# Attention outputs moved within their slot, and the hi/lo split of the last two ordinary weight passes dealt to other engines

## The chip, the cores and the metric

The kernel runs on one core of a Trainium2 chip. The metric is the device time of one execution in microseconds (us), lower is better; every quoted time is a median of several executions or comes from one profiled execution, and the text says which.

## The reference

An attention block with a compressive memory feeds a mixture of four dense experts.

```python
# B, H, S, D = 4, 8, 576, 64
scores = q @ k^T / 8, causal;  a = softmax(scores);  local = a @ v
q_p = elu(q) + 1
mem_out = (q_p @ M_prev) / (q_p . z_prev + 1e-6)
x = g * mem_out + (1 - g) * local          # g = sigmoid(beta), one per head
# x is laid out as 2304 rows of 512; E = 4 experts, F = 1024
out = sum over e of p[:, e] * (relu(x @ w1[e]) @ w2[e])
```

All data are 32-bit floats. The kernel keeps that precision with a split: a value is rounded to a short "hi" (type fp32r) and a remainder "lo" = value - hi, and each product is three matmuls (hi·hi, hi·lo, lo·hi).

## The kernel before, in words

**Attention as steps.** Attention is cut into tasks of two heads. A first run for batch 0 is written out by hand; then come 12 *joint* tasks (query chunks 0 and 1 of both heads, four slots each) and 16 others (five slots each). Every operation of a task is an event with a slot number and a priority within the slot; sorted by both, the events make one static list, and each engine executes its instructions in exactly that order. The table `PR` holds these slots and priorities. For a joint task that begins at slot s, the scores of its chunks (`j_qk`) stand at s and s+2 with priority 0; the output product (`j_o`) stands at s+6, and that is the third slot of the next task. In that slot of the next task one finds, by priority: `j_o` of the old task (-0.2), `j_qk` of the new task's second chunk (0), the query remainders `lo_q` of the task after that (0.4), the exponentials (6.5), the transposes of the first chunk (`j_pt`, 7). One slot earlier stand `trqp` (the transposes of the memory queries, 2.5), `lo_qp` (their remainders on VectorE, lines 371 and 374, written to `qpa` and `qpb`, 4.5) and `trq` (6.5). The PSUM tag `to` has two buffers; `trk`, `trqp`, `trq` and `j_o` take them in turn, so `j_o` takes the buffer that `trqp` had, and this one is free when `lo_qp` has read it.

**Experts as passes.** Between the steps lies the expert work. A pass `i` handles one half of one expert's F for one or two groups of 256 rows: `mm1` (line 851, 16 parts of three matmuls) and `mm2` (line 881, four parts for each block of 128 rows). The groups start at passes 0, 5, 8, 13 and 16; pass 23 is the last of this kind (`PH0` is 24). A pacing rule releases attention steps according to the TensorE cost of the parts done; a step with TensorE work counts as its cost plus 1500, another as 400.

**Weights.** `w_prep` makes hi and lo of a 128x512 piece of weights. The remainder is always a subtraction on Pool (line 249). The hi is either a copy on ScalarE (line 246) or a multiply by one on Pool (line 248). The pieces are staged by DMAs on SyncE's queue in four buffers (`stg`), and a buffer is loaded again when Pool has made its remainder.

**The last part.** From pass 22 on there are no attention steps left. During passes 22 and 23, seven operands of the remaining 1024 rows are made (`x_ops`: A11, S1, S2, S4, S3, A12, A22, each 128x1024; four of them need a sum first, line 994): `put` makes the hi on ScalarE (line 986) and the lo on VectorE (line 987). Before pass 24, `wt_prep` makes combinations of its weights twice (p = 0 and 1), with sums and remainders on VectorE (lines 1021 to 1030) and hi on ScalarE (lines 1025 to 1027). Passes 24 to 31 (the tail) then run `tail_mm1` (line 1046; products go to PSUM banks X, Y and Z, and ScalarE evicts the first of each, line 1057) and `tail_mm2` (line 1097).

Of the kernel before, what the change touches and what calls it, by code (L numbers as in the profile page):

```python
# [10 lines left out]
AF = mybir.ActivationFunctionType  # L11
# [11 lines left out]
PR = {  # L23
    "phi1": [-5, 1],
    "phi2": [-5, 7],
    "phi3": [-4, 7],
    "trq": [-3, 6.5],
    "trk": [-4, -0.5],
    "v": -2,
    "trqp": [1, 2.5],  # L30
    "qk": 0,
# [6 lines left out]
    "jn": [1, -0.45],  # L38
    "jp": [2, 7],
    "jlo": 9,  # L40
    "jo": [4, -0.2],
    "wpe": 1500,
    "wvec": 400,
    "frac": 0.97,
# [13 lines left out]
def tile_attention_moe(  # L58
# [13 lines left out]
    nc = tc.nc  # L72
# [39 lines left out]
    START = [g // 2 * NPH + (PR["x"] if g % 2 else 0) for g in range(NG)]  # L112
    PH0 = START[-1] + NPH
# [20 lines left out]
    def f(ap):  # L134
        return ap.bitcast(F32)

    def rows(c):
        return min(P, S - c * P)
# [86 lines left out]
    def w_more():  # L225

        while wpos["due"]:
            wpos["due"] -= 1
            w_dma()

    def w_prep(i, kind, pool=False):

        act = (kind == "1" or i < START[1]) and i < PH0 - PR["ahead"] and not pool
        j = wpos["prep"]
        if j >= len(wseq) or wseq[j][0] != i or wseq[j][1] != kind:
            return
        w_more()
        wpos["prep"] += 1
        fc = wseq[j][2]
        t = stg.pop(j)  # L240
        hi, lo = (w1s if kind == "1" else w2s)[fc]
        if kind == "1":
            hi = hi.rearrange("p c f -> p (c f)")
            lo = lo.rearrange("p c f -> p (c f)")
        if act:
            nc.scalar.activation(hi, t, AF.Copy)  # L246
        else:
            nc.gpsimd.tensor_scalar(hi, t, 1.0, 1.0, ALU.mult, ALU.mult)  # L248
        nc.gpsimd.tensor_tensor(lo, t, f(hi), ALU.subtract)  # L249
        wpos["due"] += 1  # L250
# [567 lines left out]
    def pcol(pieces):  # L818
        b, c = pieces[0]
        return 4 * b + c if c < 4 else 4 * B + b // 2  # L820
# [47 lines left out]
    def mm2(i, g, tt, after):  # L868
        e = halves[i][0]
        pieces = GROUPS[g][tt]  # L870
        pe = pn[:, pcol(pieces), e : e + 1]
        t0 = (g % 2) * GW + tt * P
        tk = slice(t0, t0 + P)
        pt = []

        def part(fc):
            if fc == 0:
                pt.append(ps.tile([P, 512], F32, tag="moe", name=f"y{i}_{g}_{tt}", bufs=3))
            wh, wl = w2s[fc]
            for z, (h_, w_) in enumerate(((hh, wh), (hh, wl), (hl, wh))):  # L880
                nc.tensor.matmul(  # L881
                    pt[0],
                    lhsT=h_[fc][:, tk],
                    rhs=w_,
                    start=(fc == 0 and z == 0),
                    stop=(fc == HF - 1 and z == 2),
                )
            if fc == HF - 1:
                fin()
                after()  # L890

        def fin():
            if i == START[g]:
                acc[g, tt] = sp.tile([P, DM], F32, tag="acc", name=f"acc{g}_{tt}", bufs=4)
                nc.vector.tensor_scalar(acc[g, tt], pt[0], pe, None, ALU.mult)
            else:
                nc.vector.scalar_tensor_tensor(  # L897
                    acc[g, tt], pt[0], pe, acc[g, tt], ALU.mult, ALU.add
                )
            if i == START[g] + NPH - 1:  # L900
                o0 = 0
                for b, c in pieces:
                    r0, m = b * S + c * P, rows(c)
                    nc.sync.dma_start(out=out[r0 : r0 + m, :], in_=acc[g, tt][o0 : o0 + m])
                    o0 += m

        return [lambda c=c: part(c) for c in range(HF)]

    def phase_parts(i):
        gs = [g for g in range(NG) if START[g] <= i < START[g] + NPH]  # L910
        c0 = min(g % 2 for g in gs) * GW
        cols = slice(c0, c0 + len(gs) * GW)
        out_ = []
        for fc in range(HF):
            for p_ in mm1(i, fc, cols, lambda: w_prep(i, "2")):
                out_.append((3 * mm(len(gs) * GW), p_))
        if i + 1 in START:
            out_.append((0.0, START.index(i + 1)))
        nt = 2 * len(gs)

        def after():
            if i + 1 == PH0:
                wt_prep(PH0)
            else:
                for _ in range(HF // nt):
                    w_prep(i + 1, "1")

        for g in gs:
            for tt in range(2):
                for p_ in mm2(i, g, tt, after):  # L930
                    out_.append((3 * mm(DM), p_))
        return out_
# [43 lines left out]
    def a_blk(i, k):  # L976
        return xt[:, 2 * k : 2 * k + 2, i * TB : (i + 1) * TB]

    def x_ops():

        X, s_ = tail["x"], tail["s"]
        s3 = tail["r"][:, 0:2]

        def put(n, src, eng):
            hi, lo = X[n]
            nc.scalar.activation(hi, src, AF.Copy)
            eng.tensor_tensor(lo, src, f(hi), ALU.subtract)

        def plain(n, i, k):
            return [lambda: put(n, a_blk(i, k), nc.vector)]  # L990

        def summed(n, eng, dst, a, b, op):
            return [
                lambda: eng.tensor_tensor(dst, a, b, op),
                lambda: put(n, dst, eng),
            ]

        return (
            plain("A11", 0, 0)
            + summed("S1", nc.vector, s_, a_blk(1, 0), a_blk(1, 1), ALU.add)  # L1000
            + summed("S2", nc.vector, s_, s_, a_blk(0, 0), ALU.subtract)
            + summed("S4", nc.vector, s_, a_blk(0, 1), s_, ALU.subtract)
            + summed("S3", nc.vector, s3, a_blk(0, 0), a_blk(1, 0), ALU.subtract)
            + plain("A12", 0, 1)
            + plain("A22", 1, 1)
        )

    def wt_prep(i):

        j = wpos["prep"]  # L1010
        if j >= len(wseq) or wseq[j][0] != i or wseq[j][1] != "1":
            return
        w_more()
        wpos["prep"] += 2
        t1, t2 = stg.pop(j), stg.pop(j + 1)
        hi, lo = tail["w"][wseq[j][2]]
        t = tail["t"]
        b11, b21, b12, b22 = t1[:, 0:GW], t1[:, GW:], t2[:, 0:GW], t2[:, GW:]
        t1 = t1.rearrange("p (n w) -> p n w", w=GW)
        gp = (nc.vector if i == PH0 else nc.gpsimd).tensor_tensor  # L1020
        gp(t[:, 0], b12, b11, ALU.subtract)
        gp(t[:, 1], b22, t[:, 0], ALU.subtract)
        gp(t[:, 2], b22, b12, ALU.subtract)
        gp(t[:, 3], b21, t[:, 1], ALU.subtract)
        nc.scalar.activation(hi[:, 0:2], t1, AF.Copy)
        nc.scalar.activation(hi[:, 2], b22, AF.Copy)
        nc.scalar.activation(hi[:, 3:7], t, AF.Copy)
        gp(lo[:, 0:2], t1, f(hi[:, 0:2]), ALU.subtract)
        nc.vector.tensor_tensor(lo[:, 2], b22, f(hi[:, 2]), ALU.subtract)
        nc.vector.tensor_tensor(lo[:, 3:7], t, f(hi[:, 3:7]), ALU.subtract)  # L1030
        wpos["due"] += 2
# [86 lines left out]
    def tail_phase(i):  # L1118
        for p in range(2):
            tail_mm1(i, p)  # L1120
            for _ in range(2):
                w_prep(i, "2")
        for t in range(0, NTL, 2):
            tail_mm2(i, (t, t + 1))
            if t < 4:
                wt_prep(i + 1)
# [247 lines left out]
    with tc.manual_schedule():  # L1374
# [43 lines left out]
        for n, ph in enumerate(phases):  # L1418
            if n == PH0 - PR["ahead"]:
                tail_init()  # L1420
                pieces = x_ops()
            for z, (cost, part) in enumerate(ph):
                if z % 3 == 2 and pieces:
                    pieces.pop(0)()
                if isinstance(part, int):
                    while si[0] < len(steps) and steps[si[0]][0] <= group_end[part]:
                        sdone += steps[si[0]][1]
                        run_step()
                    x_split(part)
                    continue  # L1430
                while si[0] < len(steps) and sdone <= target(done):
                    sdone += steps[si[0]][1]
                    run_step()
                part()
                done += cost
# [36 lines left out]
```

## Time and profile before

| | |
|---|---|
| median of 3 executions | 1090.19 us (1086.31 to 1091.47) |
| the profiled execution | 1091.35 us, its span 1089.6 us |
| mean granted TensorE clock | 0.966 |
| busy in the span | TensorE 93%, VectorE 62%, Pool 51%, ScalarE 50% |

A span is what the profiler sees from the first to the last instruction. In a line of the trace, "PE" is TensorE's matmuls, "PEld" its weight loads, "DVE" VectorE, "ACT" ScalarE, "POOL" Pool and "SP" SyncE's DMA queue. An "idle before" tells how long the engine stood before that instruction and whose end released it. TensorE's clock has two levels, 2.4 and 1.2 GHz; a granted clock of 1.00 in a stretch is the upper level throughout.

### The profile page before, as it was taken

The numbers are of one execution on the slowest core, as the hardware profiler recorded it, in microseconds if no ns is written. First come the engines' busy times: TensorE is split into PE (matmuls) and PEld (weight loads), VectorE is DVE, ScalarE is ACT, GpSimd is POOL, SyncE is SP. The second block draws the span as 40 slices with busy tenths as digits, with TensorE's granted clock in tenths as the row PEclk, the third lists the DMA queues.
The fourth block names the chain that finished last, engine by engine and source line by source line (L and its number), as shares of the span: only waits on it lengthen the run. The fifth ranks groups of instructions, "written<-read, shape, count | busy, mean of one in ns | idle before, by whom it ended". The sixth has DMA issues, their size and how long they took to land.

```text
span 1089.6 us, 15735 instructions
## 1 busy us (share of the span) xinstructions
PE 1013.7 (93%) x5072; PEld 841.2 (77%) x5072; DVE 678.4 (62%) x1606; ACT 540.8 (50%) x1231; POOL 558.3 (51%) x609
## 2 busy tenths in 40 slices
PE   6876877987999999999999999977999999999998
PEld 3666766776888887888888888856888888888886
DVE  6776676767776777777777777456534534534533
ACT  4565554555766676666766666423322422422420
POOL 5757464554556545666455555396534334334320
PEclk9988788998999999999999999988999999999999
DMA  5546435254453443453444342233221112111102
GB/s 135 135 122 155 114 101 135 82 138 109 125 131 92 122 114 104 131 149 100 120 123 124 92 130 76 79 108 115 76 58 58 39 59 58 39 58 59 39 20 77
DMA packets 192513, 106.33 MB, mean 98 GB/s; under 512 B 99632, under 2 KB 170800, under 8 KB 192432
## 3 DMA queue, kind: packets, MB, share of 16 engines
q1 hardware_dynamic: 191760, 105.07, 36.1%
q8 instruction: 40, 0.66, 0.3%
q10 hardware_dynamic: 672, 0.27, 0.1%
q14 instruction: 41, 0.34, 0.1%
HBM read 90.09 MB, written 4.72 MB: 87 GB/s over the span
## 4 chain that ended last, share of the span: by engine, by line
PE 71%; DVE 13%; POOL 6%; issue 5%; ACT 2%; DMA 1%; SPq 1%; POOLq 0%; ACTq 0%; DVEq 0%
PE yt L1097 16%; PE y L881 15%; PE h L851 12%; PE tc_1X L1046 4%; PE tc_0X L1046 4%; PE pt L359 3%; PE sp L613 3%; PE o L724 3%; POOL w2l L249 2%; PE tc_1Y L1046 2%; PE tc_0Y L1046 2%; DVE s L522 1%; POOL w1l L249 1%; DVE hl L861 1%; PE o L557 1%
## 5 line engine op out<-in xcount | busy, mean ns | idle before, releaser
L249 POOL TENSOR_TENSOR w1l<-stg,w1h 128x512 fp32r<-128x512 f32 x96 | 127.0, 1327 | 218.2 <-ACT w1h L246 210.5
L249 POOL TENSOR_TENSOR w2l<-stg,w2h 128x512 fp32r<-128x512 f32 x128 | 167.6, 1310 | 30.7 <-ACT w2h L246 21.4
L851 PE MATMUL h<-xh,w1h 128*128 128x512 f32 (+1 forms) x384 | 150.4, 392 | 0.1
L851 PE MATMUL h<-xh,w1l 128*128 128x512 f32 (+1 forms) x384 | 139.6, 364 | 2.3 <-POOL w1l L249 2.3
L881 PE MATMUL y<-w2h,hh 128*128 128x512 f32 x320 | 141.1, 441 | 0.5 <-POOL w2h L248 0.3
L851 PE MATMUL h<-xl,w1h 128*128 128x512 f32 (+1 forms) x384 | 139.1, 362 | 0.0
L881 PE MATMUL y<-w2l,hh 128*128 128x512 f32 x320 | 131.5, 411 | 7.1 <-POOL w2l L249 7.1
L881 PE MATMUL y<-w2h,hl 128*128 128x512 f32 x320 | 130.5, 408 | 0.0
L861 DVE SCALAR_TENSOR_TENSOR hl<-h,hh 128x512 fp32r<-128x512 f32 (+1 forms) x96 | 57.7, 601 | 77.9 <-ACT hh L860 77.0
L248 POOL TENSOR_SCALAR w2h<-stg 128x512 fp32r<-128x512 f32 x112 | 73.4, 655 | 58.1 <-PE yt L1097 45.2
L1110 DVE SCALAR_TENSOR_TENSOR xt<-yt,pn,xt 128x512 f32<-128x512 f32 x56 | 42.0, 751 | 87.0 <-PE yt L1097 87.0
L656 ACT ACTIVATE s<-s,st 128x384 f32<-128x384 f32 (+2 forms) x80 | 55.0, 688 | 70.4 <-DVE st L651 70.1
L851 PEld LDWEIGHTS h<-xh,w1l 128*128 128x128 f32 x384 | 74.7, 195 | 14.0 <-POOL w1l L249 2.9
L851 PEld LDWEIGHTS h<-xh,w1h 128*128 128x128 f32 x384 | 75.2, 196 | 6.8 <-POOL w1h L248 0.3
L851 PEld LDWEIGHTS h<-xl,w1h 128*128 128x128 f32 x384 | 75.4, 196 | 5.4
L897 DVE SCALAR_TENSOR_TENSOR acc<-y,pn,acc 128x512 f32<-128x512 f32 x70 | 52.3, 746 | 42.5 <-PE y L881 42.1
L881 PEld LDWEIGHTS y<-w2l,hh 128*128 128x128 f32 x320 | 63.3, 198 | 18.3 <-POOL w2l L249 11.3
L860 ACT ACTIVATE hh<-h 128x512 fp32r<-128x512 f32 (+1 forms) x96 | 50.3, 524 | 51.7 <-PE h L851 50.6
L881 PEld LDWEIGHTS y<-w2h,hl 128*128 128x128 f32 x320 | 62.9, 197 | 14.2 <-DVE hl L861 0.4
L881 PEld LDWEIGHTS y<-w2h,hh 128*128 128x128 f32 x320 | 63.2, 197 | 10.8 <-POOL w2h L248 2.5
L359 PE MATMUL pt<-ident,s 128*128 128x128 f32 (+1 forms) x376 | 61.6, 274 | 9.1 <-DVE s L522 5.8
L359 PEld LDWEIGHTS pt<-ident,s 128*128 128x128 f32 (+1 forms) x376 | 45.7, 139 | 28.4 <-issue 10.0
(297 smaller groups left out, 2601.4 us busy)
## 6 DMA issues: line engine op xcount, KB each, us to landing
stg<-in_moe_w_dram SPq DMA_DIRECT2D x256, 256.0 KB, 2.9
natall<-in_k_dram SPq DMA_DIRECT2D x34, 128.0 KB, 2.7
natall<-in_v_dram SPq DMA_DIRECT2D x32, 128.0 KB, 3.1
natall<-in_q_dram SPq DMA_DIRECT2D x60, 64.0 KB, 2.6
out_dram<-acc SPq DMA_DIRECT2D x10, 256.0 KB, 2.1
kha<-kha SPq DMA_DIRECT2D x16, 128.0 KB, 2.3
khb<-khb SPq DMA_DIRECT2D x16, 128.0 KB, 2.4
natall<-in_k_dram SPq DMA_DIRECT2D x28, 64.0 KB, 2.5
```

What stands on the lines that cost most here:

```text
L248: nc.gpsimd.tensor_scalar(hi, t, 1.0, 1.0, ALU.mult, ALU.mult)
L249: nc.gpsimd.tensor_tensor(lo, t, f(hi), ALU.subtract)
L359: nc.tensor.transpose(dst, src, ident[0:n, 0:n])
L656: nc.scalar.activation(s.s[:, 0:w], s.s[:, 0:w], AF.Copy, scale=s.st[:, 3:4])
L851: nc.tensor.matmul(pt[0][:, cols], lhsT=w_[:, c], rhs=x_[:, c, cols], start=(c == 0 and z == 0), stop=(c == NKD - 1 and z == 2),)
L860: nc.scalar.activation(h_, pt[0][:, cols], AF.Relu)
L861: nc.vector.scalar_tensor_tensor(l_, pt[0][:, cols], 0.0, f(h_), ALU.max, ALU.subtract)
L881: nc.tensor.matmul(pt[0], lhsT=h_[fc][:, tk], rhs=w_, start=(fc == 0 and z == 0), stop=(fc == HF - 1 and z == 2),)
L897: nc.vector.scalar_tensor_tensor(acc[g, tt], pt[0], pe, acc[g, tt], ALU.mult, ALU.add)
L1046: nc.tensor.matmul(bank[b][:, 0:TB], lhsT=w_[:, n, cs], rhs=x_[:, c], start=first and c == 0 and z == 0, stop=c == 1 and z == 2, skip_grou ...
L1097: nc.tensor.matmul(o, lhsT=h_[fc][:, tk], rhs=w_, start=(z == 0 and fc == p and y == 0), stop=(z == 1 and fc == p + 2 and y == 2),)
L1110: nc.vector.scalar_tensor_tensor(acc_, o, pe, acc_, ALU.mult, ALU.add)
```

## The change

Three things are changed. The priority of `j_o` goes from -0.2 to 3, so that it comes behind `j_qk` and `lo_q` of the same slot. In passes 22 and 23 the hi of both kinds of weights is made by ScalarE and no longer by Pool, and in exchange `put` makes the hi of the seven operands on VectorE, so that these are made there alone. And the first `wt_prep` of pass 24 is issued after the first part of pass 23's `mm2` instead of at the end of its first block (the second one then falls to the end of that block).

```diff
-    "jo": [4, -0.2],
+    "jo": [4, 3],
...
     def w_prep(i, kind, pool=False):
 
-        act = (kind == "1" or i < START[1]) and i < PH0 - PR["ahead"] and not pool
+        act = (kind == "1" or i < START[1] or PH0 - PR["ahead"] <= i < PH0) and not pool
...
+            if fc == 0 and i + 1 == PH0 and tt == 0:
+                wt_prep(PH0)
             if fc == HF - 1:
                 fin()
                 after()
...
         def put(n, src, eng):
             hi, lo = X[n]
-            nc.scalar.activation(hi, src, AF.Copy)
+            eng.tensor_copy(hi, src)
             eng.tensor_tensor(lo, src, f(hi), ALU.subtract)
```

## Rows read from the trace of the kernel before

**Rows 1.** Two lines of the page's second part (40 slices of 27.2 us each; busy tenths of TensorE, and its granted clock in tenths).

```profile
PE   6876877987999999999999999977999999999998
...
PEclk9988788998999999999999999988999999999999
```

**Rows 2.** Busy time by stretch: its bounds and length, then the busy time (and number of instructions) of PE, PEld, DVE, ACT and POOL, the granted clock, the DMA share and GB/s.

```profile
60.00:280.00 220.00, 179.66 (x934) 152.70 (x934) 150.87 (x409) 117.32 (x312) 121.82 (x142) 0.88 0.45 119
69.11:168.64 99.53, 78.49 (x424) 68.94 (x424) 66.64 (x175) 53.19 (x144) 58.37 (x64) 0.84 0.45 120
200.00:220.00 20.00, 17.05 (x91) 13.55 (x91) 16.15 (x47) 11.57 (x33) 12.27 (x15) 1.00 0.43 118
...
715.20:757.50 42.30, 32.20 (x139) 23.54 (x138) 26.69 (x30) 11.73 (x19) 35.70 (x28) 0.80 0.35 100
```

**Rows 3.** Who waited for whom, first TensorE from 40 to 300 us, then VectorE from 60 to 280 us: total us, times, the longest.

```profile
PE o L553 <- DVE qpb L374: 34.5, 11, 5.1
PE pt L359 <- DVE s L522: 5.8, 4, 3.6
...
DVE hl L861 <- ACT hh L860: 27.8, 11, 4.9
DVE s L486 <- PE sp L481: 24.2, 7, 6.1
```

**Rows 4.** TensorE in order of time, the first matmul of `j_o` in four of the eleven joint tasks whose `j_o` waited, the first and the last among them (start, duration; idle before and releaser in brackets).

```profile
69.11 0.55 PE L553 MATMUL o<-qpa,ms 128*128 128x256 f32 x1 [5.06 <-DVE qpb L374]
...
204.76 0.36 PE L553 MATMUL o<-qpa,ms 128*128 128x256 f32 x1 [1.11 <-DVE qpb L374]
...
219.51 0.36 PE L553 MATMUL o<-qpa,ms 128*128 128x256 f32 x1 [1.84 <-DVE qpb L374]
...
251.55 0.55 PE L553 MATMUL o<-qpa,ms 128*128 128x256 f32 x1 [2.03 <-DVE qpb L374]
```

**Rows 5.** VectorE in order of time over one joint task, from one `lo_qp` to the next (left-out lines in between have no idle time in front of them).

```profile
108.26 0.43 DVE L374 SCALAR_TENSOR_TENSOR qpb<-tp,qpb 64x256 fp32r<-64x256 f32 x1
...
112.45 0.42 DVE L861 SCALAR_TENSOR_TENSOR hl<-h,hh 128x256 fp32r<-128x256 f32 x1 [3.30 <-ACT hh L860]
114.12 0.42 DVE L486 CUSTOM_DVE_ANT_0 s<-sp,mask 128x256 f32<-128x256 f32 x1 [1.25 <-PE sp L481]
...
115.71 0.42 DVE L861 SCALAR_TENSOR_TENSOR hl<-h,hh 128x256 fp32r<-128x256 f32 x1 [0.81 <-ACT hh L860]
...
117.48 0.42 DVE L543 TENSOR_TENSOR ptl<-pt,pth 128x256 fp32r<-128x256 f32 x1 [0.47 <-ACT pth L542]
...
126.10 2.27 DVE L522 TENSOR_SCALAR s<-s,st 128x128 f32<-128x128 f32 x2
...
128.81 0.43 DVE L374 SCALAR_TENSOR_TENSOR qpb<-tp,qpb 64x256 fp32r<-64x256 f32 x1
```

**Rows 6.** TensorE in the same task: `j_o`, the first of the nine expert matmuls behind it, the second chunk's scores, and the first chunk's transposes.

```profile
108.84 0.55 PE L553 MATMUL o<-qpa,ms 128*128 128x256 f32 x1 [3.81 <-DVE qpb L374]
...
111.00 0.52 PE L851 MATMUL h<-xh,w1h 128*128 128x256 f32 x1
...
113.03 0.41 PE L481 MATMUL sp<-kha,qa 128*128 128x256 f32 x1
...
115.45 0.38 PE L359 MATMUL pt<-ident,s 128*128 128x128 f32 x2
```

**Rows 7.** Pool in order of time, passes 22 and 23 (first and last of a chain of 32 operations without idle time, and some between).

```profile
710.79 0.62 POOL L248 TENSOR_SCALAR w1h<-stg 128x512 fp32r<-128x512 f32 x1
...
715.42 2.15 POOL L249 TENSOR_TENSOR w1l<-stg,w1h 128x512 fp32r<-128x512 f32 x1
717.54 1.59 POOL L248 TENSOR_SCALAR w1h<-stg 128x512 fp32r<-128x512 f32 x1
...
750.78 1.28 POOL L249 TENSOR_TENSOR w2l<-stg,w2h 128x512 fp32r<-128x512 f32 x1
```

**Rows 8.** VectorE in order of time in the same stretch: operand remainders and sums, the first of the weight sums of the first `wt_prep`, and the `acc` behind its last operation.

```profile
715.19 1.22 DVE L987 TENSOR_TENSOR A11l<-xt,A11h 128x1024 fp32r<-128x1024 f32 x1
...
735.41 2.30 DVE L994 TENSOR_TENSOR trow<-xt 128x1024 f32<-128x1024 f32 x1
...
753.38 0.75 DVE L897 SCALAR_TENSOR_TENSOR acc<-y,pn,acc 128x512 f32<-128x512 f32 x1 [7.60 <-PE y L881]
754.05 0.42 DVE L1021 TENSOR_TENSOR tsum<-stg,stg 128x256 f32<-128x256 f32 x1
...
757.86 0.75 DVE L897 SCALAR_TENSOR_TENSOR acc<-y,pn,acc 128x512 f32<-128x512 f32 x1
```

**Rows 9.** TensorE in order of time, the wait in pass 23 for Pool's last remainder, and the first matmul that waited in pass 24.

```profile
752.12 0.80 PE L881 MATMUL y<-w2l,hh 128*128 128x512 f32 x1 [0.30 <-POOL w2l L249]
...
761.70 0.50 PE L1046 MATMUL tc_0X<-S2h,wth 128*128 128x512 f32 x1 [1.27 <-ACT trow L1057]
```

**Rows 10.** ScalarE in order of time, its last copy for the second `wt_prep` and its first eviction in pass 24.

```profile
760.10 1.06 ACT L1027 ACTIVATE wth<-tsum 128x1024 fp32r<-128x1024 f32 x1 [2.30 <-DVE tsum L1024]
761.07 0.58 ACT L1057 ACTIVATE trow<-tc_0X 128x512 f32<-128x512 f32 x1
```

**Rows 11.** VectorE in order of time, two normalizations that nothing delays (each line is two instructions, and the time is that of both).

```profile
211.63 0.62 DVE L522 TENSOR_SCALAR s<-s,st 128x256 f32<-128x256 f32 x2
...
218.01 0.48 DVE L522 TENSOR_SCALAR s<-s,st 128x128 f32<-128x128 f32 x2
```

## The prediction, made before the changed kernel was run

> **What bounds the kernel now.** I read the page first. TensorE is busy in nine tenths or more of a slice from 300 us on and less before, and there is one dent at slices 26 and 27; the granted clock sags at the same places [rows 1]. Where it is full, TensorE alone sets the pace, and work taken from another engine gives nothing. The busy times by stretch say how much: from 60 to 280 us TensorE works 179.7 of 220 us at a clock of 0.88, and from 715.2 to 757.5 it works 32.2 of 42.3 us at 0.80 [rows 2]. The view of waits names the first loss: TensorE waited 34.5 us, eleven times, in front of `j_o`, each time for VectorE's `qpb`, and for little else [rows 3]. The order of instructions tells why. `j_o` takes the `to` buffer of `trqp`, which `lo_qp` must have read, and `lo_qp` is VectorE's last work of a long run. So the wait belongs to a loop: VectorE ends `lo_qp`, TensorE runs `j_o`, nine expert matmuls, and only then the second chunk's scores, for which VectorE in the meantime has nothing to do. In the task of [rows 5] `lo_qp` ends at 108.69; VectorE idles 3.30, 1.25, 0.81 and 0.47 us, comes to the first chunk's remainder (`ptl`) at 117.48, 8.8 us after `lo_qp`, and from there works without a pause for 11.8 us until the next `lo_qp` ends at 129.24. The loop is 20.55 us long.
>
> The dent is Pool's. In passes 22 and 23 its chain of 32 operations runs unbroken from 710.79 to 752.06 [rows 7], and TensorE's matmuls of `mm2` wait for one remainder after the other, last at 752.12 [rows 9]. A hi and a lo undisturbed cost 0.62 + 1.29 us, 1.96 with gaps, so 16 pairs would take 31.4 us; they take 41.3. The 9.9 us more are eleven operations that take 0.9 us longer (1.59 for 0.62, 2.15 for 1.29), each beside one of VectorE's eleven operations on two 128x1024 operands in SBUF, which in turn go from 1.22 to as much as 2.30 us [rows 7, 8]. The two engines take turns there.
>
> **Part 1, `j_o` behind `j_qk` and `lo_q`.** Nothing is added or removed. In pacing units `j_o` comes 1937 + 400 later, `j_qk` and `lo_q` 2583 earlier; since today 2583 units between `j_o` and `j_qk` hold nine matmuls of 256 columns [rows 6], about as much expert work will now stand between `j_qk` and `j_o`. VectorE's own order of the attention work stays; ScalarE's copy of the output still comes before the exponentials. `j_o` issues no DMA. `lo_q` brings two DMAs (query halves) earlier past SyncE's queue; their readers come half a task later.
>
> *Bound from below: only the local swap.* TensorE has the scores and about nine expert matmuls to do before it stands at `j_o`. The nine took 2.03 us from 111.00 to 113.03, at the lower clock, 0.23 each; thirteen are 2.9 us at that level and 1.5 at the upper one. I take 1.7 us. If `lo_qp` ends no earlier, each wait shrinks by that much: ten waits by 1.7 and the one of 1.11 wholly, 18 us.
>
> *With the loop.* Scores stand ready when `lo_qp` ends, so VectorE goes on at once. Then `j_o` takes 1.1 to 2.2 us (108.84 to 111.00 at the lower level, half of it at the upper), nine expert matmuls 1.0 to 2.0, the transposes and ScalarE's copy of them about 1 (today 2.0, from 115.45 to 117.48, with two exponentials in front) [rows 5, 6]: `ptl` can begin 3.2 to 5.1 us after `lo_qp` instead of 8.8. Meanwhile VectorE has 2.1 us of its own to do (scores 0.85, `lo_q` 0.85, one `hl` 0.42). I take 4.2 us. With the unbroken 11.8 the loop is 16.0 us. TensorE then comes to `j_o` some 14 to 15.5 us after the last `lo_qp`, so it still waits there, 0.5 to 2 us. The first five loops, from 69.11 to 168.64, are 99.5 us together [rows 2, 4]; 5 x 16.0 is 80, a gain of 19.5. The next five, to 251.55, are 82.9 us. Among them is one that began after a short wait (1.11 us) and whose clock stayed at 1.00: 204.76 to 219.51, 14.75 us [rows 2, 4]. 5 x 14.75 is 73.8, a gain of 9.1. The first wait itself, 5.06 us, loses 1.7. Sum: 30 us. Bound from above: all ten loops at 14.75, 1.84 less for the wait inside, 12.9 us each: 182.4 - 129 + 2 = 55 us, which leaves VectorE (66.6 of 99.5 us busy in the first five, 13.3 each) no slack, so I don't go near it.
>
> **Part 2, passes 22 and 23.** Pool loses 16 hi (16 x 0.66 us with gaps), so its 16 remainders alone would be done by about 732 undisturbed. ScalarE gains 16 copies of 128x512 and loses seven of 128x1024, nearly as many columns; it is busy 11.7 of 42.3 us [rows 2], so this hides under its idle time. Without that cover the thousand columns more, some 1.1 us by [rows 10], would count. VectorE gains seven copies of 128x1024, and with it the bound moves. No row has this copy. The nearest is the normalization, 0.31 us for 128x256 and 0.24 for 128x128 [rows 11], so 0.07 for each 128 columns: 0.73 us; the other end is the two-operand 1.22 us [rows 8]. I take 0.73, since it is the same kind of operation, one SBUF operand.
>
> VectorE's work from 715.2 to the last sum of the second `wt_prep`: 11 x 1.2 + 7 x 0.73 + 8 `hl` x 0.42 + 3 `acc` x 0.75 + 3.8 (first `wt_prep`, 754.05 to 757.86 [rows 8]) + 1.6 (four sums) = 29.3 us, which ends at 744.5. ScalarE's last copy and first eviction (1.06 and 0.58 [rows 10]) make it 746.2; that eviction is what TensorE waited for at 761.70 [rows 9]. Now the turns with Pool. Thirteen remainders of 1.28 us fall into this time, 16.6 us; those that run beside `hl` and `acc`, which leave Pool alone, cost VectorE nothing (about 4.9 us). VectorE waits the other 11.7 (a normalization took 2.27 us in place of 0.48 [rows 5, 11], so work with one operand in SBUF can be held up too). 757.9 instead of 761.7: a gain of 4. Bounds: no waits at all, 15; copies of 1.22 and no wait hidden, 766.2, a loss of 5. The later `hl` then is what `mm2` waits for in both passes, and no longer Pool.
>
> That copies on VectorE take a turn with Pool at all is also what the Trainium skill says (SBUF — State Buffer, "Who interferes with whom"): a copy between SBUF tiles may run over both ports and then holds the pair that Pool needs, while ScalarE's ports are its own; it speaks against moving these seven there. By that rule the gain is the 4 us of the sum; if the copies took one port and no turn, seven waits of at most 0.9 us would go and it would be about 8.
>
> **Part 3, `wt_prep` earlier.** Its VectorE work no longer stands behind the `acc` of 753.38, which idled 7.60 us for TensorE [rows 8]. That is inside the sum above. One weight load moves ahead of one output DMA on SyncE; neither is awaited for several us.
>
> **Sum.** 1091.35 - 30 - 4 = 1057 us. That is against the profiled execution, 1.2 us above the median; its 1.75 us outside the span stay.
>
> **The rivals.** *Swap only*: VectorE's run grows to fill the loop, as much of it waits for Pool and not for scores. For it: 2.27 us of normalization [rows 5]. Against it: the idle time stands right behind `lo_qp`, 52 us in all [rows 3]. 1091 - 18 - 4 = 1069 us. *The wait moves on*: TensorE waits as long at the transposes behind `j_o` (they waited 5.8 us [rows 3]). Against it: their operand is normalized before `lo_qp`. Then part 2 alone, 1087 us. *All of it*: with waits below 1.1 us the clock stays up throughout, loops of 14.0 us, 42 + 8 us: 1041. *Slower, by the clock*: the lower clock holds through the loops. A loop holds 12.9 us of TensorE work at the upper level (14.75 - 1.84); once more than 5.3 us of it run at half rate, 18.2 us (the mean of today's ten) is exceeded; all of it would be 25.8, +76 us in ten loops, 1163. Against it: after the wait of 1.11 us the clock stood at 1.00, and shorter waits are what is forecast [rows 2, 4].
>
> **How the numbers follow.** Forecast 0.47 (own range 1047 to 1064), swap only 0.25 (1063 to 1078), all of it 0.15, the wait moves on 0.08, slower 0.05. The range of 1040 to 1080 leaves out the last two and part of "all of it". Faster by over 0.5% (5.4 us, about what can be told from no change) 0.88; within it 0.07, the cases near 1087; slower 0.05.
>
> **What would show it.** Waits of `j_o` for `qpb` under 18 us in all, and VectorE's idle time behind `lo_qp` (52 us) under 20; loops of 14 to 17 us; the clock over 0.93 from 60 to 250. In passes 22 and 23, no Pool multiply, remainders done ten us or more before the tail, seven VectorE copies near 0.7 us or up to 2 where Pool is in turn, and `mm2` waiting for `hl`. It is wrong if `j_o` waits as long as before, or the transposes take over the wait, or the first tail matmul that waits comes no earlier relative to the start of pass 22 than now (761.70 less 714.3).

## The result, and the profile after

The changed kernel takes 1061.7 us (median of 4 executions, 1060.47 to 1062.96) against 1090.7 us (the median of four executions of the kernel before): a ratio of 0.9742, with a 95% interval from 0.9714 to 0.9771. The prediction was 1057 us. The profiled execution took 1062.06 us, its span 1060.3 us, 29.3 us less than the span of before, at a mean clock of 0.977.

Two lines of the page's second part, which answer to [rows 1] (slices of 26.5 us, counted from 0): the dent at slices 26 and 27 is still there, and one slice shorter in its clock.

```profile
PE   5887888998999999999999999978999999999998
...
PEclk8989889999999999999999999989999999999999
```

In what follows, `hh` and `hl` are the hi and lo of the hidden layer that `mm2` takes, `acc` adds up `mm2`'s outputs, `pth` and `ptl` are the hi and lo of a chunk's transposed weights of attention, `otmp` is ScalarE's copy of `j_o`'s output, and `st` holds the statistics of the rows, their reciprocals among them.

Busy time by stretch, columns as in [rows 2]: the first five loops of the joint tasks, the next five, and the whole joint stretch.

```profile
69.45:160.94 91.49, 76.26 (x427) 65.23 (x427) 68.58 (x176) 54.01 (x145) 58.03 (x64) 0.89 0.48 131
160.94:233.28 72.34, 67.61 (x359) 55.44 (x359) 59.81 (x168) 43.35 (x119) 45.01 (x60) 0.98 0.49 130
60.00:250.00 190.00, 163.86 (x894) 137.42 (x895) 150.18 (x397) 112.20 (x301) 116.43 (x137) 0.93 0.50 134
```

Both groups of loops became shorter, though not alike. The first five went from 99.5 to 91.5 us (-8.0), the next five from 82.9 to 72.3 (-10.6), and the last one, up to the twelfth `j_o`, from 21.6 to 18.4 (-3.2). The first `j_o` starts 0.3 us later. Up to the twelfth `j_o` that makes 21.5 us. `j_o` itself has changed its place, though; the end of VectorE's twelfth `lo_qp`, which has not, went from 273.72 to 251.04, 22.7 us.

Who waited for whom, first TensorE from 40 to 280 us, then VectorE from 60 to 250; they answer to [rows 3].

```profile
PE o L553 <- DVE qpb L374: 17.8, 10, 3.5
PE pt L359 <- DVE s L522: 4.6, 4, 2.6
...
DVE hl L861 <- ACT hh L860: 13.2, 7, 3.8
DVE acc L899 <- PE y L881: 10.3, 5, 4.4
DVE ptl L543 <- ACT pth L542: 7.3, 6, 1.4
```

TensorE's wait in front of `j_o` is halved (34.5 to 17.8 us). VectorE's wait for the scores, 24.2 us before, is gone. But VectorE still waits 30.8 us in these three rows, 28.4 of them between a `lo_qp` and the next `ptl`, for work of TensorE or ScalarE.

The end: the `acc` that ends pass 21 starts at 691.82 instead of 714.53 (-22.7), and the first tail matmul that waits comes 40.4 us after it instead of 47.2 (-6.8). TensorE in order of time, first two waits of pass 22, then the matmul that answers to the second of [rows 9]:

```profile
703.68 0.79 PE L881 MATMUL y<-w2h,hl 128*128 128x512 f32 x1 [3.12 <-DVE hl L861]
707.57 0.79 PE L881 MATMUL y<-w2h,hl 128*128 128x512 f32 x1 [2.25 <-DVE hl L861]
...
732.21 0.50 PE L1049 MATMUL tc_0X<-S2h,wth 128*128 128x512 f32 x1 [1.19 <-ACT trow L1060]
```

As forecast, `mm2` now waits there for VectorE's `hl` (8.4 us in four waits from 690 to 735) and hardly for Pool (0.6 us, once). VectorE in order of time, the operands S1 and S3; these lines answer to [rows 8], with the new copies (L989):

```profile
697.43 1.44 DVE L989 CAST S1h<-xsum 128x1024 fp32r<-128x1024 f32 x1
698.90 2.18 DVE L990 TENSOR_TENSOR S1l<-xsum,S1h 128x1024 fp32r<-128x1024 f32 x1
...
714.18 0.68 DVE L989 CAST S3h<-trow 128x1024 fp32r<-128x1024 f32 x1
714.90 1.23 DVE L990 TENSOR_TENSOR S3l<-trow,S3h 128x1024 fp32r<-128x1024 f32 x1
```

Pool in the same stretch, four remainders to a line; this answers to [rows 7], and no multiply is left among them:

```profile
694.23 7.98 POOL L249 TENSOR_TENSOR w2l<-stg,w2h 128x512 fp32r<-128x512 f32 x4 [1.11 <-ACT w2h L246]
702.17 8.36 POOL L249 TENSOR_TENSOR w1l<-stg,w1h 128x512 fp32r<-128x512 f32 x4
715.92 6.98 POOL L249 TENSOR_TENSOR w2l<-stg,w2h 128x512 fp32r<-128x512 f32 x4 [5.38 <-ACT w2h L246]
```

From 710.5 to 715.9 Pool stands still, and just there S3's copy and remainder take 0.68 and 1.23 us. Beside Pool's remainders the same operations take 1.44 and 2.18, and a remainder of Pool takes about 2.0 us instead of 1.29. The copies take turns with Pool too. That agrees with the rule of the Trainium skill named in the prediction (SBUF — State Buffer, "Who interferes with whom").

### The profile page after: what moved, and what is told of

Same layout as the page of the kernel before. It is cut to its first block, busy times and chain, and to the rows that moved or that the text cites. A ratio compares the mean times of both kernels' runs of the same rounds, so it can differ in the third digit from the quotient of the medians.

```text
span 1060.3 us, 15727 instructions
## 1 busy us (share of the span) xinstructions
PE 998.6 (94%) x5072; PEld 830.6 (78%) x5072; DVE 691.1 (65%) x1613; ACT 542.2 (51%) x1240; POOL 545.7 (51%) x593
## 4 chain that ended last, share of the span: by engine, by line
PE 74%; DVE 14%; POOL 3%; ACT 3%; issue 2%; DMA 2%; SPq 1%; ACTq 0%; POOLq 0%; DVEq 0%
PE y L881 17%; PE yt L1100 16%; PE h L851 13%; PE tc_1X L1049 4%; PE tc_0X L1049 4%; PE pt L359 3%; PE o L724 3%; PE sp L613 3%; PE tc_1Y L1049 2%; PE tc_0Y L1049 2%; DVE s L522 2%; DVE hl L861 1%; DMA stg<-in_moe_w_dram 1%; POOL w2l L249 1%; PE tc_0Z L1049 1%
## 5 line engine op out<-in xcount | busy, mean ns | idle before, releaser
L249 POOL TENSOR_TENSOR w2l<-stg,w2h 128x512 fp32r<-128x512 f32 x128 | 170.5, 1334 | 30.8 <-ACT w2h L246 22.1
L881 PE MATMUL y<-w2l,hh 128*128 128x512 f32 x320 | 128.6, 402 | 2.9 <-POOL w2l L249 2.9
L248 POOL TENSOR_SCALAR w2h<-stg 128x512 fp32r<-128x512 f32 x104 | 65.2, 627 | 58.2 <-PE yt L1100 45.2
L851 PEld LDWEIGHTS h<-xh,w1h 128*128 128x128 f32 x384 | 74.5, 194 | 7.2 <-ACT qb L368 0.6
```

The lines of the kernel that those rows point to most:

```text
L851: nc.tensor.matmul(pt[0][:, cols], lhsT=w_[:, c], rhs=x_[:, c, cols], start=(c == 0 and z == 0), stop=(c == NKD - 1 and z == 2),)
L881: nc.tensor.matmul(pt[0], lhsT=h_[fc][:, tk], rhs=w_, start=(fc == 0 and z == 0), stop=(fc == HF - 1 and z == 2),)
```

## The experiments

Ratios are to the kernel before on the same chip (its medians there were 1091.6 to 1092.2 us). Diffs are against the changed kernel.

**Do the parts add?** The first run keeps only the new place of `j_o`, the second only the change at the end.

```diff
-        act = (kind == "1" or i < START[1] or PH0 - PR["ahead"] <= i < PH0) and not pool
+        act = (kind == "1" or i < START[1]) and i < PH0 - PR["ahead"] and not pool
...
-            if fc == 0 and i + 1 == PH0 and tt == 0:
-                wt_prep(PH0)
...
-            eng.tensor_copy(hi, src)
+            nc.scalar.activation(hi, src, AF.Copy)
```

> Only the priority of j_o is changed, the rest is as before. Theory (the two parts are independent, and the joint tasks give most): the stretch up to the start of pass 22 is shorter by about 22.7 us, as in the changed kernel, and the end of the span by no more: about 1068 us. Rival (the parts help one another, for example because Pool and ScalarE come earlier to the weights): 1072 us or more, with the sum of the two parts alone short of the 29 us.

```diff
-    "jo": [4, 3],
+    "jo": [4, -0.2],
```

> j_o stays at -0.2; the hi and lo of passes 22 and 23 and the early wt_prep are as in the changed kernel. Theory: 6 to 7 us faster than before, about 1084 us, all of it between the acc that ends pass 21 and the first tail matmul that waits (47.2 us before, 40.4 in the changed kernel). Rival (the end gives nothing by itself, since VectorE only takes Pool's place): within 2 us of before.

The first took 1068.21 us (ratio 0.9783 [0.9765, 0.9801]), the second 1083.3 (0.9928 [0.9912, 0.9944]). Their spans are 23.2 and 8.7 us shorter than that of before, 31.9 together, and both changes at once give 29.3. The stretch from the end of pass 21 to the first waiting tail matmul is 47.2 us long in the first run and 40.5 in the second. So the parts lie in different stretches and add to within 3 us.

**What the copies on VectorE are worth.** Only `put`'s hi goes back to ScalarE:

```diff
-            eng.tensor_copy(hi, src)
+            nc.scalar.activation(hi, src, AF.Copy)
```

> The changed kernel, but the hi of the seven operands is made on ScalarE again, beside its weight copies. Theory (VectorE and its turns with Pool bound passes 22 and 23, and the seven copies on it only cost): VectorE loses seven copies of 0.7 to 1.5 us, some 8 us, gets three waits for ScalarE of about 0.8 us each; the stretch from the end of pass 21 to the first waiting tail matmul goes from 40.4 to about 35 us, the time to about 1057. Rival (ScalarE, which now has both kinds of copies in its order, holds up the weights' hi, which wait behind copies that wait for VectorE's sums): 40 us or more in that stretch, 1062 to 1066 us.

It took 1055.05 us (0.9668 [0.9654, 0.9681]), faster than the changed kernel. The stretch at the end went from 40.4 to 36.3 us. Who waited for whom there, TensorE from 688 to 728 us:

```profile
PE y L881 <- POOL w2l L249: 3.2, 4, 1.1
...
PE y L881 <- ACT w2h L246: 1.0, 1, 1.0
PE y L881 <- DVE hl L861: 0.9, 1, 0.9
```

The waits for `hl` fell from 8.4 to 0.9 us, and short waits for Pool and ScalarE took their place. The copies on VectorE are thus a loss of 4.1 us: without them the end would have given 10.9 us and not 6.8. The other 2.2 us by which this span is shorter arose before pass 21 ended, where the two kernels are the same; profiled executions of kernels that are the same up to there reached that point at 691.82, 689.62 and 689.18 us (the changed kernel, this run and the next). Differences of two us before that point are therefore not read as an effect.

**The early `wt_prep`.** Only its new place is undone:

```diff
-            if fc == 0 and i + 1 == PH0 and tt == 0:
-                wt_prep(PH0)
```

> The changed kernel without the early wt_prep: it is issued at the end of pass 23's blocks again. Theory (its VectorE work then stands behind the acc that waits for the end of mm2's first block): the first wt_prep's 3.8 us come behind that acc, about 4 us later than now, and the first waiting tail matmul 3 to 4 us later: 1065 us. Rival (the second wt_prep and ScalarE's eviction decide alone, and these move little): 1062 us.

It took 1061.3 us (1057.4 to 1066.5; 0.9731 [0.9705, 0.9757]), the same as the changed kernel. TensorE's first waiting matmul of the tail:

```profile
731.43 0.69 PE L1047 MATMUL tc_0X<-S2h,wth 128*128 128x512 f32 x1 [2.48 <-ACT trow L1058]
```

The wait is 2.48 us instead of 1.19, and the stretch 42.3 us instead of 40.4. The early place is worth some 2 us there, less than the 3 to 4 expected, and the total time can't resolve it.

**Which part of `j_o`'s move counts.** Behind the scores, but still ahead of the query remainders:

```diff
-    "jo": [4, 3],
+    "jo": [4, 0.2],
```

> The changed kernel with j_o at priority 0.2: behind the scores, but ahead of lo_q. Theory (what counts is that the second chunk's scores stand ahead of j_o, so that VectorE has work when lo_qp ends; lo_q has no TensorE work): within 3 us of the changed kernel, 1060 to 1065, and VectorE does not wait for scores. Rival (the query remainders and their DMAs, moved ahead, give the gain): 1070 us or more.

1062.61 us (0.9739 [0.9724, 0.9754]): the same as with 3. The scores ahead of `j_o` are what counts; `lo_q` does not matter. `j_o` waits 19.5 us in eleven waits.

Still later, behind the exponentials and the first chunk's transposes:

```diff
-    "jo": [4, 3],
+    "jo": [4, 8],
```

> The changed kernel with j_o at priority 8: behind the exponentials and the first chunk's transposes too. In the changed kernel VectorE comes to the first chunk's remainder some 6 us after lo_qp in the first five loops, where 4.2 were forecast, since the transposes and the expert matmuls it waits for stand behind j_o, which runs at the lower clock after its wait. Theory (that is why the first five loops are 18.3 us and not 16.0): with the transposes ahead of j_o this wait goes too, j_o waits for qpb under 5 us in all, the first five loops take 15 to 16.5 us each, the time is 1046 to 1055. Rival (VectorE's run itself, with its turns with Pool, bounds these loops): the waits of j_o go, but the loops stay near 18 us, 1058 to 1063; or j_o's late output holds the buffer that the next transposes need, and new waits there eat the gain.

1046.73 us (0.959 [0.9576, 0.9604]), another 15 us. Busy time by stretch, again the first and the next five loops:

```profile
69.14:152.21 83.07, 71.89 (x423) 59.20 (x424) 69.58 (x176) 53.85 (x145) 58.32 (x64) 0.96 0.53 144
152.21:218.46 66.25, 65.12 (x359) 54.55 (x359) 59.50 (x170) 45.21 (x121) 45.35 (x60) 1.00 0.54 141
```

Who waited for whom, TensorE from 60 to 250 us:

```profile
PE pt L359 <- DVE s L522: 11.0, 11, 2.9
...
PE o L553 <- DVE qpb L374: 1.3, 4, 0.6
```

The wait for `qpb` is all but gone, the clock is at 0.96 and 1.00, and the loops take 16.6 and 13.25 us, 8.4 and 6.1 us in all less than in the changed kernel; the 16.6 is just above the 15 to 16.5 expected. A wait at the transposes takes its place in part.

This leaves two suspects for what had held the changed kernel's loops back: ScalarE's exponentials or TensorE's transposes, both of which stood behind `j_o`. The next place lets only the exponentials ahead:

```diff
-    "jo": [4, 3],
+    "jo": [4, 6.8],
```

> The changed kernel with j_o behind the next tile's exponentials but ahead of its transposes (due 6.8 in place of 4). It tells which of the two that due 8 let ahead gives the 15 us. Theory (TensorE's transposes and what follows them stood behind the wait for qpb): near the changed kernel, 1057 to 1062, waits of j_o for qpb 14 to 18 us. Rival (ScalarE's exponentials stood behind ScalarE's share of j_o): near the run with due 8, 1045 to 1050, though j_o still waits for qpb.

1053.53 us (0.9637 [0.9607, 0.9667]), between the two expectations: by the medians 8.2 us come with this place, 6.8 more with the place behind the transposes. The loops themselves divide it a little differently. Busy time by stretch in this run, the first and the next five loops:

```profile
69.48:158.01 88.53, 74.52 (x424) 63.95 (x424) 66.55 (x176) 54.67 (x145) 58.51 (x64) 0.91 0.50 135
158.01:226.88 68.87, 66.00 (x358) 54.14 (x359) 59.17 (x168) 44.41 (x121) 45.29 (x60) 1.00 0.52 134
```

In the ten loops this place gave 6.4 us, and the place behind the transposes another 8.1. Part of each step is the clock: in the first five loops about the same number of TensorE's matmuls took 78.5 us in the kernel before, 76.3 in the changed one, 74.5 here and 71.9 with 8, at clocks of 0.84, 0.89, 0.91 and 0.96.

TensorE's and ScalarE's waits from 60 to 250 us in this run:

```profile
PE o L553 <- DVE qpb L374: 15.2, 10, 3.5
...
ACT s L500 <- DVE st L486: 31.3, 17, 4.9
```

and ScalarE's in the changed kernel:

```profile
ACT otmp L571 <- PE o L557: 34.1, 10, 6.9
ACT s L500 <- DVE st L486: 16.4, 10, 2.5
```

In the changed kernel ScalarE waited 34.1 us for `j_o`'s products, which it copies to `otmp`. In the kernel before, whose joint tasks last longer, it had been, from 60 to 275 us:

```profile
ACT otmp L571 <- PE o L557: 44.2, 11, 6.9
```

The change took away less than a quarter of that wait, where it halved TensorE's. With 6.8 it is not among ScalarE's seven largest waits any more (the seventh is 3.8 us), and the kernel is faster although `j_o` itself waits nearly as long as before (15.2 us). So what a wait costs is not only its own length but also what stands in order behind it on every engine that takes part. The run doesn't isolate the exponentials, though: each of them that goes ahead of `j_o` also lets expert work through by the pacing rule, and in the first three loops TensorE now does 1536, 3072 and 2304 columns of expert matmuls between `j_o` and the transposes, instead of 3072, 3840 and 3072. How much of the gain is ScalarE's order and how much TensorE's was not told apart.

**Is it VectorE's run that bounds the loop?** The joint tasks' normalizations take up to 2.3 us where Pool takes turns with them [rows 5]. They go to ScalarE, which leaves VectorE's run shorter, once with the new and once with the old place of `j_o`:

```diff
-            nc.vector.tensor_scalar(s.s3[:, hd], s.s3[:, hd], r[:, hd : hd + 1], None, ALU.mult)
+            nc.scalar.activation(s.s3[:, hd], s.s3[:, hd], AF.Copy, scale=r[:, hd : hd + 1])
```

> The changed kernel with the joint tasks' normalizations made by ScalarE (48 instructions; on VectorE they take 0.65 us on average, about 2.6 us for each loop). If VectorE's run from the first chunk's remainder to lo_qp bounds the loops: up to 2.6 us from each of the first five and 1 to 2 from the others, 10 to 20 us, 1042 to 1052. If the waits for work behind j_o bound them: VectorE has more idle time and the loops shorten by under 1 us, 1055 to 1062.

> The same with j_o back at -0.2. It shows whether a shorter VectorE run alone takes the wait at j_o away: then 15 to 25 us faster than with j_o at -0.2 and VectorE's normalizations (1083 with the end as changed), 1058 to 1068. If the order is what makes the loop, VectorE's idle time behind lo_qp grows by as much as the run shrinks only in part: the loop loses up to 2.6 us, eleven times at the most, and its idle time for scores (24 us) stays: 1065 to 1075.

1077.47 us (0.9863 [0.9842, 0.9884]) and 1105.22 (1.0126 [1.0105, 1.0147]): 16 and 22 us slower than the kernels that differ only in this, the changed one and the second run (1083.3). Neither idea foresaw this. Who waited for whom in the first of them from 60 to 250 us, ScalarE and then VectorE:

```profile
ACT s L522 <- DVE st L516: 49.2, 21, 3.6
...
DVE hl L861 <- ACT hh L860: 18.2, 13, 2.3
DVE qp L330 <- ACT ex L325: 14.6, 8, 2.0
DVE qpa L371 <- ACT qpb L368: 11.4, 9, 1.5
```

ScalarE now waits 49.2 us for VectorE's reciprocals (`st`), and everything behind the normalization in its order is late: `hh`, the exponentials of `ex`, the copies of the memory queries. VectorE in turn waits for those. The handing over cost more than the work that it saved. The runs say nothing on a shorter run on VectorE by itself.

**Both edits that helped.** `put`'s hi on ScalarE and `j_o` behind the transposes:

```diff
-    "jo": [4, 3],
+    "jo": [4, 8],
...
-            eng.tensor_copy(hi, src)
+            nc.scalar.activation(hi, src, AF.Copy)
```

> The changed kernel with both edits that made it faster: put makes the hi of the last pass's operands on ScalarE, and j_o stands behind the next tile's exponentials and transposes (due 8). Theory (the two gains lie in different stretches and add): 1046.7 less the 6 that the first edit gave, 1040 to 1042; the stretch from the accumulation that ends pass 21 to the first waiting tail matmul about 36, the waits of j_o for qpb under 2 us. Rival (the later j_o has already moved the loops so that the end waits for other work): 1044 to 1047, with the end stretch at 39 or more.

1042.93 us (0.954 [0.952, 0.9561]). The stretch at the end is 36.3 us (677.50 to 713.79), 4.1 less than with `j_o`'s move alone, as in the third run, and `j_o` waits 1.3 us. The gain lies where it was expected. Its size was overestimated: 1040 to 1042 counted the 2.2 us that belong to no edit. This is the fastest version, 19 us below the changed kernel and 49 below the one before.

And one slot later still, again with `put`'s hi on ScalarE:

```diff
-    "jo": [4, 3],
+    "jo": [5, -0.5],
...
-            eng.tensor_copy(hi, src)
+            nc.scalar.activation(hi, src, AF.Copy)
```

> As the run with both edits, and j_o a whole slot later, behind the next slot's scores. Theory (the later place pays only as long as it takes a wait of j_o away; 1.3 us of that wait is left): within 4 us of the run with both edits. Rival 1 (a later joint output holds the buffer of the joint's outputs and the stores that follow it): slower by 5 or more, and a wait for it in VectorE's or TensorE's rows. Rival 2 (TensorE's transposes, which waited 11.9 us for s in the run with due 8, find s ready): faster by 5 or more.

1042.75 us (0.9541 [0.9523, 0.956]): the same. Once the wait is gone, a later place gives nothing and, here, costs nothing.

## Why the prediction was right, and which term was off

The measured 1061.7 us lies in the forecast's own range of 1047 to 1064, and both mechanisms are the ones named. Its sum, 30 us from the joint tasks and 4 from the end, came out as 22.7 and 6.8. That the total fell into the range is partly luck: the two misses have opposite signs, and 22.7 with the 4 forecast for the end would have given 1064.7.

**The loop, right in form.** The prediction wrote a loop as the time from `lo_qp` to `ptl` plus VectorE's unbroken run. In the five first loops of the changed kernel `ptl` starts 7.1, 8.0, 4.85, 6.4 and 6.1 us after `lo_qp` ends, 6.5 on average. VectorE's run from there to the end of the next `lo_qp` is 11.8 us on average, as the prediction had it, and the sum is the 18.3 us of a loop. (The single runs differ: in the loop below it is 14.0 us.) In the kernel before, the same five loops had 8.1 and 11.8. So the gain, 1.6 us a loop, came from the time ahead of `ptl` alone. The prediction's 8.8 was that of one loop, longer than their average.

**The term that was mis-sized: `ptl` at 4.2 us after `lo_qp`.** It cost 5 x 2.3 = 11.5 us, the whole difference between the 19.5 us forecast and the 8.0 measured. The working took `j_o`, nine expert matmuls (2304 columns), and then "about 1" for the transposes, their copy and what stands ahead of it. Both parts were too small. In the five loops 3072, 3840, 3072, 2304 and 3072 columns of expert matmuls lie between `j_o` and the transposes (and only 1536 in four of the five between the scores and `j_o`), so the transposes start 4.05 us after `lo_qp` on average and not 3.2; and from there to `ptl` it is 2.4 us and not 1. One loop of the changed kernel shows it, first ScalarE in order of time:

```profile
125.92 0.77 ACT L571 ACTIVATE otmp<-o 64x256 f32<-64x256 f32 x2 [4.12 <-PE o L557]
126.71 0.51 ACT L500 ACTIVATE s<-s,st 128x256 f32<-128x256 f32 x1
...
127.22 0.50 ACT L500 ACTIVATE s<-s,st 128x256 f32<-128x256 f32 x1
...
128.38 0.38 ACT L542 ACTIVATE pth<-pt 128x256 fp32r<-128x256 f32 x1 [0.57 <-PE pt L359]
129.02 0.38 ACT L860 ACTIVATE hh<-h 128x256 fp32r<-128x256 f32 x1 [0.26 <-PE h L851]
```

then VectorE from one `lo_qp` to the next:

```profile
122.95 0.43 DVE L374 SCALAR_TENSOR_TENSOR qpb<-tp,qpb 64x256 fp32r<-64x256 f32 x1
...
129.43 0.42 DVE L861 SCALAR_TENSOR_TENSOR hl<-h,hh 128x256 fp32r<-128x256 f32 x1 [3.25 <-ACT hh L860]
129.77 0.41 DVE L543 TENSOR_TENSOR ptl<-pt,pth 128x256 fp32r<-128x256 f32 x1
...
143.34 0.43 DVE L374 SCALAR_TENSOR_TENSOR qpb<-tp,qpb 64x256 fp32r<-64x256 f32 x1
```

and TensorE:

```profile
123.52 0.55 PE L553 MATMUL o<-qpa,ms 128*128 128x256 f32 x1 [2.85 <-DVE qpb L374]
...
127.71 0.63 PE L359 MATMUL pt<-ident,s 128*128 128x128 f32 x2
...
129.77 0.28 PE L851 MATMUL h<-xh,w1l 128*128 128x256 f32 x1
```

After `lo_qp` ends at 123.38, `j_o` takes 2.2 us at the lower clock. ScalarE, which waited 4.12 us for it, then copies the output (0.77), runs two exponentials (1.1), waits 0.57 us more for the transposes, which TensorE does two us after `j_o`, and makes `pth` and one `hh`; VectorE's `hl` needs that `hh` and stands ahead of `ptl`. Together that is 6.4 us, and only at its end are TensorE's expert matmuls back at 0.28 us, from 0.41 to 0.42 behind `j_o`.

Here the exponentials themselves cost nothing, since ScalarE had still to wait for the transposes behind them. `pth` in the other four loops, in order of time, and a wait of ScalarE in the second of them:

```profile
74.95 0.38 ACT L542 ACTIVATE pth<-pt 128x256 fp32r<-128x256 f32 x1 [1.21 <-PE pt L359]
...
90.18 0.63 ACT L246 ACTIVATE w2h<-stg 128x512 fp32r<-128x512 f32 x1 [5.19 <-DMA stg<-in_moe_w_dram]
...
95.00 0.37 ACT L542 ACTIVATE pth<-pt 128x256 fp32r<-128x256 f32 x1
...
111.20 0.37 ACT L542 ACTIVATE pth<-pt 128x256 fp32r<-128x256 f32 x1
...
149.41 0.38 ACT L542 ACTIVATE pth<-pt 128x256 fp32r<-128x256 f32 x1 [0.17 <-PE pt L359]
```

In three of the five loops (1.21, 0.57 and 0.17 us of idle time) TensorE's order held `pth` up; in the two others `pth` followed ScalarE's exponentials without a wait, in one of them after ScalarE had stood 5.19 us for a weight DMA. So ScalarE's order, which the prediction had read and not priced, is one part of the missing time and TensorE's the other. The runs with 6.8 and with 8 agree: the 6.5 us became 5.5 with the exponentials ahead of `j_o` and 3.6 with the transposes ahead too. What VectorE does between `ptl` and the next `lo_qp` grew to 12.2 and 13.0 there, so part of what the shorter wait gave was taken back.

**The next five loops** gave 10.6 us for the 9.1 forecast: the model loop of 14.75 us, read from a stretch at the full clock, held (14.5). The last loop gave 3.2 us that the sum did not count. The first wait did become 1.7 us shorter, but its `j_o` came no earlier.

**The end: 6.8 us instead of 4.** The bound moved to VectorE as forecast. Its work from the end of that `acc` to the last sum of the second `wt_prep` was set at 29.3 + 11.7 = 41.0 us; it took 38.1 (692.49 to 730.59). The turns with Pool cost 10.3 us: 6.3 in eleven two-operand operations (19.76 us against 11 x 1.22) and 4.0 in seven copies (8.74 against 7 x 0.68). The rest is smaller because operations in sequence overlap: an `hl` of 0.42 us holds the next one up by only 0.33. The copy alone was right (0.68 us for the estimate of 0.73), and six of seven took 1.1 to 1.46. The prediction had a reason against having these copies on VectorE, and did not ask what they would cost there compared with ScalarE, though they lie on the chain that bounds the stretch. The third run prices that: 4.1 us lost.

**The rivals.** "Swap only" (18 us from the joint tasks) is nearer to the 22.7 measured than the forecast's 30 is, and the first five loops gave 1.6 us each where it says 1.7 for each wait. But its mechanism did not come: VectorE's run did not grow there (11.8 us on average before and after), and what filled the loop was the 6.5 us ahead of it. "The wait moves on" to the transposes did not happen (4.6 us after, 5.8 before, over all joint tasks), but came true in part at 8 (11.0 us) at a gain. "All of it" (1041) is nearly what the best version shows, with waits of 1.3 us, but that version has two more edits. "Slower by the clock" is refuted: from 60 to 250 us the clock is at 0.93, where it was 0.87 before.

**The signs.** Waits of 17.8 us (under 18), no Pool multiply, a copy at 0.68 us and `mm2` waiting for `hl` came as said; the clock of 0.93 is just at its mark. Three missed. The first five loops, at 18.3 us, lie above 14 to 17. VectorE's idle time behind `lo_qp` is 30.8 us, not under 20. Pool's remainders ended at 722.9, some 5 us ahead of the tail's start at 728.1 instead of ten.

With 8 the span up to the `acc` that ends pass 21 is 16.1 us shorter than in the changed kernel, though the twelfth `j_o` comes only 12.6 us earlier. The difference is in the mark: with 8, `j_o` stands behind more work of its slot. VectorE's twelfth `lo_qp`, whose place is the same, in the changed kernel and with 8:

```profile
250.55 0.49 DVE L374 SCALAR_TENSOR_TENSOR qpb<-tp,qpb 64x320 fp32r<-64x320 f32 x1
...
235.07 0.49 DVE L374 SCALAR_TENSOR_TENSOR qpb<-tp,qpb 64x320 fp32r<-64x320 f32 x1
```

It comes 15.5 us earlier, so nearly all of the gain lies in the joint tasks. What stays open is how the gain of the place behind the exponentials divides between ScalarE's order and TensorE's, and what a shorter run on VectorE would be worth by itself.

## What to carry to other kernels

When an instruction waits, list what stands in order behind it on each engine that takes its result, not only on its own; here ScalarE's copy of the waiting product stood ahead of exponentials that had nothing to do with it, and TensorE's transposes stood behind the product. With the exponentials ahead, the kernel became 8.2 us faster while the product's own wait shrank by only 2.6 us. Move such an instruction back until its wait is gone; here one slot more was then neither gain nor loss. And before dealing work to another engine, ask which engine's chain bounds that stretch: copies moved onto it cost 4 us, although a copy alone is shorter there (0.68 us) than where it came from (1.05).

## What the runs showed of the hardware that was not expected

A copy of 128x1024 from fp32 to fp32r between SBUF tiles takes 0.68 us on VectorE with Pool idle and up to 1.46 us beside Pool's subtractions (four of seven took 1.43 to 1.46); on ScalarE it is 1.04 to 1.06 us in the kernel before and in the third run, beside the same subtractions. So beside a busy Pool the engine that is faster alone is the slower one.

A normalization that VectorE does in 0.48 to 2.3 us cost 16 and 22 us in all when the joint tasks' normalizations went to ScalarE, where, in the run that cost 16, they waited 49.2 us for VectorE's reciprocals in 21 waits; how much of the cost is that wait and how much the longer queue was not told apart.
